# A SwiGLU block on one core: x turned by VectorE in 32x32 blocks, from loads by quarters of its columns

## The chip, the cores and the metric

The kernel runs on one core of a Trainium2 chip. The metric is device time in microseconds. Three runs of the kernel before took 163.49, 163.84 and 164.01 us; their median, 163.84 us, is what the changed kernel is held against. The profiled execution had a span of 162.2 us on core 0, at a granted TensorE clock of 1.000.

## The reference

All tensors are bf16: x is 1 x 2048 x 640, w_gate and w_up are 640 x 1536, w_down is 1536 x 640.

```python
g = silu(x @ w_gate)
u = x @ w_up
return (g * u) @ w_down
```

In what follows S = 2048 is the row count, D = 640 the width, F = 1536 the inner width.

## The kernel before, in words

The rows are worked off in four blocks `sb` of 512. The inner width is cut into KF = 12 chunks `fc` of 128, and the width D into KD = 5 pieces `kd` of 128. The contraction of the first two products runs over D, so x must lie with D on the partitions: the tile `xT` holds it, 128 partitions by 5 by 2048.

For each block and each chunk, `proj` (L193) makes five matmuls into a PSUM tile `pg` (gate) and five into `pu` (up), each with a 128 x 128 weight and 512 columns of `xT`. `gate` (L208) then runs Silu on ScalarE from `pg` into `sg` and multiplies `sg` by `pu` on VectorE into the tile `aT`. The PSUM tiles `pg` and `pu` share four buffers (tag `gu`), so a chunk's matmuls need buffers that the Silu or the multiplication of an earlier chunk has released. `sg` has three buffers.

When a block's twelve chunks are done, the down projection follows. Its last 128 output columns are made transposed in `po_t` (L270), copied by ScalarE to `ot_t`, turned on VectorE into `ot_q` (L281) and stored in four pieces by ScalarE's queue. Its first 512 columns come in four row groups `j`, each twelve matmuls into `po_a` (L299), a copy to `ot` on ScalarE (L308) and a store on SP's queue (L317). `po_a` and `po_t` have two buffers each.

The last T = 4 rows of x are left out of the gate and up matmuls of the last block. VectorE computes them instead, as 96 "dots" (L148), each a product of one turned weight chunk (`wgT` or `wuT`, loaded by the DMA crossbar, L132) with one of these rows (`x_row`, L137), summed along 640 elements. `do_dots(n)` places n dots at points of the loops: two after the gate of a chunk in blocks 1 to 3, except the last two chunks, three before `ot_q`, three after each `po_a` copy with j above 0.

x comes in three ways. Row groups 0 and 1 (128 rows each) are loaded as they are into `x_sb` (L86), turned on TensorE with an identity (`transpose_chunk`, L181) and copied to `xT` (L191). Row groups 2 and 3, and blocks 1, 2 and 3, come through the DMA crossbar straight into `xT` (`turn_x`, L108). Block 1 is asked for after `w_down`; blocks 2 and 3 after block 0's output stores.

The head (L217) is written out by hand: 18 warm-up matmuls `pw` on a tile of ones, the ten transposes, two more warm-ups, then gate matmuls of chunks 0 and 1 by pieces of rows (L237), the up matmuls of rows 0 to 255, and the rest of rows 256 to 511. The order of instructions on TensorE and ScalarE is pinned for the head only; afterwards the scheduler places them. On VectorE and SP, `keep_order` (L98) keeps the written order through the whole kernel. Loads go out on the queues of SP and ScalarE. Their completions use eight semaphores in turn, so a DMA waits for the completion of the one eight before it, whichever of the two queues it was on.

The weights come in chunk groups W_CHUNKS: chunks 0-1, 2-3, 4-7 and 8-11, gate and up each (L83, L120).

Of the kernel before, what the change touches and what calls it, by code (L numbers as in the profile page):

```python
# [7 lines left out]


@with_exitstack  # L10
def _body(
# [8 lines left out]
    nc = tc.nc  # L20
    P = nc.NUM_PARTITIONS
    f32 = mybir.dt.float32
    bf16 = mybir.dt.bfloat16
# [15 lines left out]
    Q = 32  # L39
    N_WARM, N_GAP = 18, 2  # L40
    T = 4
    WT_STEP = 4
    PE_X = 2
    K_CUT = 2
    ROW_J = 0
    W_CHUNKS = [(0, 2), (2, 4), (4, 8), (8, 12)]
    assert D % P == 0 and F % P == 0 and S % S_BLK == 0 and D > DA and SUB == 4

    consts = ctx.enter_context(tc.tile_pool(name="consts", bufs=1))
    work = ctx.enter_context(tc.tile_pool(name="work", bufs=3))  # L50
    outp = ctx.enter_context(tc.tile_pool(name="outp", bufs=3))
    psum = ctx.enter_context(
        tc.tile_pool(name="psum", bufs=2, space=bass.MemoryType.PSUM)
    )

    ident = consts.tile([P, P], bf16)
    x_sb = consts.tile([P, PE_X, D], bf16)
    xT = consts.tile([P, KD, S], bf16)
    wg_sb = consts.tile([P, KD, F], bf16)
    wu_sb = consts.tile([P, KD, F], bf16)  # L60
# [7 lines left out]
    row_s = consts.tile([P, KF, T], f32)  # L68
    prod = consts.tile([P, D], f32)

    make_identity(nc, ident[:])

    x_v = x2.rearrange("(c p) d -> p c d", p=P)
    xt_v = x2.rearrange("s (kd p) -> s kd p", p=P)
    wg_v = w_gate.rearrange("(kd p) f -> p kd f", p=P)
    wu_v = w_up.rearrange("(kd p) f -> p kd f", p=P)
    wd_v = w_down.rearrange("(kf p) d -> p kf d", p=P)

    def wslice(a, b):
        return slice(a * P, b * P)  # L80

    def load_w(eng, dst, src, a, b):
        eng.dma_start(out=dst[:, :, wslice(a, b)], in_=src[:, :, wslice(a, b)])  # L83

    def load_x(eng, c0, c1):
        eng.dma_start(out=x_sb[:, c0:c1, :], in_=x_v[:, c0:c1, :])  # L86

    def issue_order(a, b):
        tc.add_manual_dep(
# [15 lines left out]
    silu_first = consts.tile([P, 1], f32)  # L105
    nc.vector.memset(ones[:], 1.0)  # L106

    def turn_x(c0, c1):  # L108
        s_sl = slice(c0 * P, c1 * P)
        nc.sync.dma_start_transpose(out=xT[:, :, s_sl], in_=xt_v[s_sl])  # L110

    load_x(nc.sync, 0, 1)
    load_x(nc.scalar, 1, 2)
    f_sl = wslice(*W_CHUNKS[0])
    for dst, src, first, second in (
        (wg_sb, wg_v, nc.sync, nc.scalar),
        (wu_sb, wu_v, nc.scalar, nc.sync),
    ):
        for eng, k_sl in ((first, slice(0, K_CUT)), (second, slice(K_CUT, KD))):
            eng.dma_start(out=dst[:, k_sl, f_sl], in_=src[:, k_sl, f_sl])  # L120
    turn_x(PE_X, SUB)
    nc.scalar.activation(silu_first[:], ones[:, 0:1], ACT.Silu)
    for a, b in W_CHUNKS[1:]:
        load_w(nc.sync, wg_sb, wg_v, a, b)
        load_w(nc.sync, wu_sb, wu_v, a, b)
    nc.sync.dma_start(out=wd_sb[:], in_=wd_v)
    wgt_v = w_gate.rearrange("d (kf p) -> d kf p", p=P)
    wut_v = w_up.rearrange("d (kf p) -> d kf p", p=P)

    def turn_w(dst, src):  # L130
        for a in range(0, KF, WT_STEP):
            nc.sync.dma_start_transpose(  # L132
                out=dst[:, a : a + WT_STEP, :], in_=src[:, a : a + WT_STEP, :]
            )

    turn_x(1 * SUB, 2 * SUB)
    nc.sync.dma_start(  # L137
        out=x_row[:],
        in_=x2[S - T : S, :].rearrange("t d -> (t d)").partition_broadcast(P),
# [26 lines left out]

    dots = row_dots()

    def do_dots(n):
        for _ in range(n):  # L170
            next(dots, None)
# [3 lines left out]
    def warm(n):  # L175
        for _ in range(n):
            nc.tensor.matmul(  # L177
                pw[:, 0:P], lhsT=ones[:], rhs=ones[:], start=True, stop=True
            )

    def transpose_chunk(c, parts):  # L181
        c_sl = slice(c * P, (c + 1) * P)
        for copy, tag, k0, k1 in parts:
            pt = psum.tile([P, k1 - k0, P], bf16, tag=tag, name="pt")
            for kd in range(k0, k1):
                nc.tensor.transpose(  # L186
                    out=pt[:, kd - k0, :],
                    in_=x_sb[:, c, kd * P : (kd + 1) * P],
                    identity=ident[:],
                )  # L190
            copy(out=xT[:, k0:k1, c_sl], in_=pt[:])  # L191

    def proj(ps, w_sb, fc, sb, c0, c1):  # L193
        for kd in range(KD):
# [22 lines left out]
    def head():  # L217

        dve, act = nc.vector.tensor_copy, nc.scalar.copy
        split = [(act, "po_a", 0, 2), (dve, "po_b", 2, KD)]
        late = PE_X * P
        (pg0, pu0), (pg1, pu1) = gu_tiles(), gu_tiles()
        warm(N_WARM)
        transpose_chunk(0, split)
        transpose_chunk(1, split)
        warm(N_GAP)  # L230
        early = [(kd, c * P, (c + 1) * P) for c in range(PE_X) for kd in range(K_CUT)]
        early += [(kd, 0, late) for kd in range(K_CUT, KD)]
        for kd, c0, c1 in early:
            for fc, pg in ((0, pg0), (1, pg1)):


                nc.tensor.matmul(  # L237
                    pg[:, c0:c1],
                    lhsT=wg_sb[:, kd, wslice(fc, fc + 1)],
                    rhs=xT[:, kd, c0:c1],  # L240
                    start=(kd == 0 and c0 == 0),
                    stop=(kd == KD - 1),
                )
        proj(pu0, wu_sb, 0, 0, 0, late)
        proj(pu1, wu_sb, 1, 0, 0, late)
        for fc, pg, pu in ((0, pg0, pu0), (1, pg1, pu1)):
            proj(pg, wg_sb, fc, 0, late, S_BLK)
            proj(pu, wu_sb, fc, 0, late, S_BLK)
            gate(pg, pu, 0, fc, S_BLK)
        keep_order(mybir.EngineType.PE)  # L250
        keep_order(mybir.EngineType.Activation)

    head()
    for sb in range(NSB):
        n_s = S_BLK if sb < NSB - 1 else S_BLK - T
        for fc in range(KF):
            if sb == 0 and fc < 2:
                continue
            pg, pu = gu_tiles()
            proj(pg, wg_sb, fc, sb, 0, n_s)  # L260
            proj(pu, wu_sb, fc, sb, 0, n_s)
            gate(pg, pu, sb, fc, n_s)
            if sb > 0 and fc < KF - 2:
                do_dots(2)


        n_t = (SUB if sb < NSB - 1 else SUB - 1) * P
# [12 lines left out]
        do_dots(3)  # L280
        nc.vector.transpose(out=ot_q[:], in_=ot_t[:])  # L281
        for q in range(P // Q):
            nc.scalar.dma_start(
                out=out2[
                    sb * S_BLK : sb * S_BLK + n_t, DA + q * Q : DA + (q + 1) * Q
                ].rearrange("(i r) c -> r i c", r=Q),
                in_=ot_q[q * Q : (q + 1) * Q, :].rearrange("r (i c) -> r i c", c=Q),
            )

        for j in range(SUB):  # L290
            s0 = sb * S_BLK + j * P
            last = sb == NSB - 1 and j == SUB - 1
            cols = [(0, DA, "po_a")]
            if last:
                cols = [(0, DA // 2, "po_a"), (DA // 2, DA, "po_a"), (DA, D, "po_b")]
            for c0, c1, tag in cols:
                po = psum.tile([P, c1 - c0], f32, tag=tag, name="po_a")
                for kf in range(KF):
                    nc.tensor.matmul(  # L299
                        po[:],  # L300
                        lhsT=aT[:, kf, s0 : s0 + P],
                        rhs=wd_sb[:, kf, c0:c1],
                        start=(kf == 0),
                        stop=(kf == KF - 1),
                    )
                ot = outp.tile([P, c1 - c0], bf16, name="ot" if c1 < D else "ot_b")
                if c1 < D:
                    nc.scalar.copy(ot[:], po[:])  # L308
                    eng = nc.sync
                else:  # L310
                    nc.vector.tensor_copy(out=ot[:], in_=po[:])  # L311
                    eng = nc.scalar
                if 0 < j and not last:
                    do_dots(3)
                if sb == NSB - 1 and j == ROW_J:
                    row_tail()
                eng.dma_start(out=out2[s0 : s0 + P, c0:c1], in_=ot[:])  # L317
        if sb == 0:
            turn_x(2 * SUB, 3 * SUB)
            turn_w(wuT, wut_v)  # L320
            turn_x(3 * SUB, 4 * SUB)
    keep_order(mybir.EngineType.DVE)
    keep_order(mybir.EngineType.SP)

# [104 lines left out]
```

## Time and profile before

| What | Value |
|---|---|
| Runs of the kernel before | 163.49, 163.84, 164.01 us; median 163.84 |
| Span of the profiled execution | 162.2 us |
| TensorE matmul busy | 159.8 us, 99% of the span |
| VectorE busy | 110.9 us, 68% |
| ScalarE busy | 42.7 us, 26% |
| DMA packets | 42441, 15.86 MB |
| SP queue | 33536 packets, 37.7% of 16 engines |
| ScalarE queue | 8896 packets, 4.1% of 16 engines |

The profiled execution's own time is recorded as its span from first to last instruction; what lies around it is not in the profile, and the median of the runs is 1.64 us above that span.

The profile's chain of waits is followed back from the last instruction; in this profile it is almost only TensorE. A group's "idle before" is time in which its engine had nothing to do, with what ended it. Times in the timeline are microseconds from the start of the span, and its columns are start, length, engine, line, operation, output and input tiles, shapes and count.

### The profile page before, as it was taken

How to read it: one execution, taken by the hardware profiler on the slowest of the kernel's cores; microseconds unless marked ns; L12 is line 12 of the kernel's file. 1: busy time of each engine (PE TensorE's matmuls, PEld its weight loads, DVE VectorE, ACT ScalarE, POOL GpSimd, SP SyncE). 2: the span in 40 equal slices, each digit the busy share in tenths (PEclk: the TensorE clock that was granted, in tenths of full speed). 3: DMA queues.
4: the chain of work that ended last, by engine and by line, in shares of the span. 5: the costliest groups of instructions: out<-in, count | busy, mean ns of one | idle time of the engine just before them, and what ended most of it. 6: DMA issues, size and time to landing. Idle time of an engine off the chain costs nothing.

```text
span 162.2 us, 2118 instructions
## 1 busy us (share of the span) xinstructions
PE 159.8 (99%) x798; PEld 77.9 (48%) x798; DVE 110.9 (68%) x249; ACT 42.7 (26%) x74; POOL 0.6 (0%) x6
## 2 busy tenths in 40 slices
PE   9999999999999999999999999999999999999995
PEld 8854444444444444444444444444444444445454
DVE  2042233599469999979919999979964999993000
ACT  5132222112222222221222322221214222222121
POOL 1000000000000000000000000000000000000000
PEclk9999999999999999999999999999999999999999
DMA  7999999994179992003110000000320000000312
GB/s 208 258 339 348 362 218 249 219 234 94 34 185 178 224 195 61 4 0 34 65 65 0 0 4 2 0 0 2 63 69 32 0 0 0 0 0 4 50 39 73
DMA packets 42441, 15.86 MB, mean 98 GB/s; under 512 B 33216, under 2 KB 42304, under 8 KB 42432
## 3 DMA queue, kind: packets, MB, share of 16 engines
q1 hardware_dynamic: 33536, 14.72, 37.7%
q10 hardware_dynamic: 8896, 1.02, 4.1%
q8 instruction: 6, 0.10, 0.2%
q14 instruction: 3, 0.02, 0.1%
HBM read 6.88 MB, written 2.62 MB: 59 GB/s over the span
## 4 chain that ended last, share of the span: by engine, by line
PE 99%; DVE 0%; issue 0%
PE pu L195 32%; PE pg L195 31%; PE po_a L299 26%; PE po_t L270 6%; PE pw L177 1%; PE pg L237 1%; PE pt L186 1%; DVE ot_b L311 0%; DVE ones L106 0%
## 5 line engine op out<-in xcount | busy, mean ns | idle before, releaser
L195 PE MATMUL pu<-xT,wu_sb 128*128 128x512 bf16 (+2 forms) x250 | 59.8, 370 | 0.0
L195 PE MATMUL pg<-xT,wg_sb 128*128 128x512 bf16 (+2 forms) x240 | 58.5, 374 | 0.0
L213 DVE TENSOR_TENSOR aT<-sg,pu 128x512 bf16<-128x512 f32 (+1 forms) x48 | 32.8, 683 | 32.8 <-PE pu L195 28.1
L212 ACT ACTIVATE sg<-pg 128x512 f32<-128x512 f32 (+1 forms) x48 | 28.6, 596 | 71.2 <-PE pg L195 68.1
L299 PE MATMUL po_a<-wd_sb,aT 128*128 128x512 bf16 (+2 forms) x216 | 42.8, 358 | 0.0
L148 DVE SCALAR_TENSOR_TENSOR prod<-wgT,x_row 128x640 f32<-128x640 bf16 x48 | 39.4, 821 | 1.1
L148 DVE SCALAR_TENSOR_TENSOR prod<-wuT,x_row 128x640 f32<-128x640 bf16 x48 | 39.4, 822 | 1.0
L195 PEld LDWEIGHTS <-wu_sb 128*128 128x128 bf16 x250 | 24.4, 98 | 27.6 <-DMA wu_sb<-in_w_up_dram 0.3
L195 PEld LDWEIGHTS <-wg_sb 128*128 128x128 bf16 x240 | 23.5, 98 | 26.9
L299 PEld LDWEIGHTS <-aT 128*128 128x128 bf16 x216 | 20.7, 98 | 21.6
L308 ACT CAST ot<-po_a 128x512 bf16<-128x512 f32 (+1 forms) x17 | 9.5, 560 | 32.0 <-PE po_a L299 20.8
L270 PE MATMUL po_t<-aT,wd_sb 128*128 128x512 bf16 (+1 forms) x48 | 10.4, 366 | 0.0
L270 PEld LDWEIGHTS <-wd_sb 128*128 128x128 bf16 x48 | 4.7, 98 | 5.1
L311 DVE CAST ot_b<-po_a 128x128 bf16<-128x128 f32 x1 | 0.3, 291 | 9.9 <-PE po_a L299 9.9
L279 ACT CAST ot_t<-po_t 128x512 bf16<-128x512 f32 (+1 forms) x4 | 2.2, 558 | 11.6 <-PE po_t L270 11.6
L148 DVE DVE_READ_ACCUMULATOR prod<-wuT,x_row 128x1 f32 x48 | 3.9, 82 | 0.0
L148 DVE DVE_READ_ACCUMULATOR prod<-wgT,x_row 128x1 f32 x48 | 3.9, 82 | 0.0
L281 DVE STREAM_TRANSPOSE ot_q<-ot_t 128x512 bf16<-128x512 bf16 (+1 forms) x4 | 2.7, 678 | 1.7 <-ACT ot_t L279 1.7
L177 PE MATMUL pw<-ones 128*128 128x128 bf16 x20 | 2.5, 313 | 0.4 <-DVE ones L106 0.4
L191 DVE COPY xT<-pt 128x384 bf16<-128x384 bf16 x2 | 0.7, 358 | 2.9 <-PE pt L186 2.9
L237 PE MATMUL pg<-xT,wg_sb 128*128 128x128 bf16 (+1 forms) x14 | 2.3, 360 | 0.0
L177 PEld LDWEIGHTS <-ones 128*128 128x128 bf16 x20 | 2.1, 148 | 0.4 <-DVE ones L106 0.4
(15 smaller groups left out, 7.6 us busy)
## 6 DMA issues: line engine op xcount, KB each, us to landing
wd_sb<-in_w_down_dram SPq DMA_DIRECT2D x1, 1920.0 KB, 14.5
out_dram<-ot SPq DMA_DIRECT2D x15, 128.0 KB, 1.7
wg_sb<-in_w_gate_dram SPq DMA_DIRECT2D x2, 640.0 KB, 7.7
wu_sb<-in_w_up_dram SPq DMA_DIRECT2D x2, 640.0 KB, 8.7
x_row<-in_x_dram SPq DMA_DIRECT2D x1, 640.0 KB, 4.7
out_dram<-ot_q ACTq DMA_DIRECT2D x12, 32.0 KB, 1.9
wg_sb<-in_w_gate_dram SPq DMA_DIRECT2D x1, 320.0 KB, 4.9
wu_sb<-in_w_up_dram SPq DMA_DIRECT2D x1, 320.0 KB, 5.4
```

The source lines that it names most:

```text
L148: nc.vector.scalar_tensor_tensor(out=prod[:], in0=wT[:, fc, :], scalar=1.0, in1=x_row[:, t, :], op0=ALU.mult, op1=ALU.mult, accum_out=acc[ ...
L177: nc.tensor.matmul(pw[:, 0:P], lhsT=ones[:], rhs=ones[:], start=True, stop=True)
L186: nc.tensor.transpose(out=pt[:, kd - k0, :], in_=x_sb[:, c, kd * P : (kd + 1) * P], identity=ident[:],)
L195: nc.tensor.matmul(ps[:, c0:c1], lhsT=w_sb[:, kd, fc * P : (fc + 1) * P], rhs=xT[:, kd, sb * S_BLK + c0 : sb * S_BLK + c1], start=(kd == 0 ...
L212: nc.scalar.activation(sg[:, 0:n_s], pg[:, 0:n_s], ACT.Silu)
L213: nc.vector.tensor_tensor(out=aT[:, fc, s0 : s0 + n_s], in0=sg[:, 0:n_s], in1=pu[:, 0:n_s], op=ALU.mult)
L237: nc.tensor.matmul(pg[:, c0:c1], lhsT=wg_sb[:, kd, wslice(fc, fc + 1)], rhs=xT[:, kd, c0:c1], start=(kd == 0 and c0 == 0), stop=(kd == KD ...
L270: nc.tensor.matmul(po_t[:], lhsT=wd_sb[:, kf, DA:D], rhs=aT[:, kf, sb * S_BLK : sb * S_BLK + n_t], start=(kf == 0), stop=(kf == KF - 1),)
L279: nc.scalar.copy(ot_t[:], po_t[:])
L281: nc.vector.transpose(out=ot_q[:], in_=ot_t[:])
L299: nc.tensor.matmul(po[:], lhsT=aT[:, kf, s0 : s0 + P], rhs=wd_sb[:, kf, c0:c1], start=(kf == 0), stop=(kf == KF - 1),)
L308: nc.scalar.copy(ot[:], po[:])
```

## The change

All of x now goes one way. It is loaded by quarters of its columns: quarter q, columns 160q to 160q+159, goes to partitions 32q to 32q+31, with row r of every 32-row group on partition 32q + r. One packet is 160 elements, 320 bytes. VectorE's block transpose (32 x 32 elements in each quarter of the partitions) then turns it into `xT`. It reads every fifth element of the 160, so partition p of piece k of `xT` is column 5p + k of x, and the gate and up weights are loaded with the matching row order (`(p kd) f`).

Row group 0 is in `xq_00`, row group 1 in `xq_01`, row groups 2 and 3 in `xq_02`; blocks 1 to 3 are `xq_1`, `xq_2`, `xq_3`. Block 0's quarters are loaded on both queues, two each; the other blocks' on SP's queue: block 1 before the weights of chunks 8-11, block 2 before `w_down`, block 3 after it. The turns of block 0 stand in the head. Those of blocks 1 and 2 stand behind the gates of block 0's chunks 5, 6, 7 and 9, 10, 11; those of block 3 in block 0's down projection, between the dots. Up weights of chunks 0-1 come in one load on SP's queue instead of two on both. The identity, the transposes on TensorE, their copies and the crossbar loads of x are gone. The 20 warm-ups all stand ahead of the first real matmul, and the gate matmuls of rows 0 to 255 go by row groups of 128 columns.

```diff
-    N_WARM, N_GAP = 18, 2
+    QN = P // Q
+    QD = D // QN
+    N_WARM = 20
-    ident = consts.tile([P, P], bf16)
-    x_sb = consts.tile([P, PE_X, D], bf16)
+    xq_0 = [consts.tile([P, SUB, QD], bf16, name=f"xq_0{c}") for c in range(2)]
+    xq_0.append(consts.tile([P, 2 * SUB, QD], bf16, name="xq_02"))
+    xq_n = [consts.tile([P, S_BLK // Q, QD], bf16, name=f"xq_{b}") for b in range(1, NSB)]
-    wg_v = w_gate.rearrange("(kd p) f -> p kd f", p=P)
-    wu_v = w_up.rearrange("(kd p) f -> p kd f", p=P)
+    wg_v = w_gate.rearrange("(p kd) f -> p kd f", kd=KD)
+    wu_v = w_up.rearrange("(p kd) f -> p kd f", kd=KD)
...
+    def load_quarter(eng, xq, q, s0, n):
+        eng.dma_start(
+            out=xq[q * Q : (q + 1) * Q],
+            in_=x2[s0 : s0 + n, q * QD : (q + 1) * QD].rearrange("(b r) j -> r b j", r=Q),
+        )
+
+    def turn(xq, s0, n, k0, k1):
+        src = xq[:].rearrange("p b (c kd) -> p kd b c", kd=KD)
+        for kd in range(k0, k1):
+            nc.vector.transpose(out=xT[:, kd, s0 : s0 + n], in_=src[:, kd])
...
+    load_halves(xq_0[0], 0, P)
+    load_first(nc.sync, wg_sb, wg_v, 0, K_CUT)
+    load_first(nc.scalar, wg_sb, wg_v, K_CUT, KD)
+    load_halves(xq_0[1], P, P)
+    load_first(nc.sync, wu_sb, wu_v, 0, KD)
+    load_halves(xq_0[2], 2 * P, 2 * P)
...
+    def load_block(i):
+        for q in (0, 2, 1, 3):
+            load_quarter(nc.sync, xq_n[i - 1], q, i * S_BLK, S_BLK)
+
+    for n, (a, b) in enumerate(W_CHUNKS[1:]):
+        if n == 2:
+            load_block(1)
         load_w(nc.sync, wg_sb, wg_v, a, b)
         load_w(nc.sync, wu_sb, wu_v, a, b)
+    load_block(2)
     nc.sync.dma_start(out=wd_sb[:], in_=wd_v)
+    load_block(3)
...
-    turn_x(1 * SUB, 2 * SUB)
...
+    def late_turns():
+        for i in range(1, NSB):
+            for kd in range(KD):
+                turn(xq_n[i - 1], i * S_BLK, S_BLK, kd, kd + 1)
+                yield
...
+    TURNS = {5: 2, 6: 2, 7: 1, 9: 2, 10: 2, 11: 1}
...
+        turn(xq_0[0], 0, P, 0, K_CUT)
+        turn(xq_0[0], 0, P, K_CUT, KD)
+        turn(xq_0[1], P, P, 0, K_CUT)
+        turn(xq_0[1], P, P, K_CUT, KD)
+        turn(xq_0[2], late, late, 0, KD)
...
-            if sb > 0 and fc < KF - 2:
+            if sb == 0:
+                do_turns(TURNS.get(fc, 0))
+            elif fc < KF - 2:
                 do_dots(2)
...
+                if sb == 0:
+                    do_turns(2 if j == 0 else 1)
                 if 0 < j and not last:
                     do_dots(3)
...
         if sb == 0:
-            turn_x(2 * SUB, 3 * SUB)
             turn_w(wuT, wut_v)
-            turn_x(3 * SUB, 4 * SUB)
```

In the changed kernel the gate multiplication stands at L231, a turn of x at L93, a quarter's load at L85, the dots at L164 and `proj` at L213.

More of the change, by code (lines that the diff above doesn't have):

```diff
@@ L6 @@
 from concourse._compat import with_exitstack
-from concourse.masks import make_identity
 @with_exitstack
@@ L39, in _body @@
     Q = 32
-    N_WARM, N_GAP = 18, 2
+    QN = P // Q
+    QD = D // QN
+    N_WARM = 20
     T = 4
     WT_STEP = 4
-    PE_X = 2
     K_CUT = 2
@@ L69, in _body @@
     prod = consts.tile([P, D], f32)
-    make_identity(nc, ident[:])
-    x_v = x2.rearrange("(c p) d -> p c d", p=P)
-    xt_v = x2.rearrange("s (kd p) -> s kd p", p=P)
-    wg_v = w_gate.rearrange("(kd p) f -> p kd f", p=P)
-    wu_v = w_up.rearrange("(kd p) f -> p kd f", p=P)
+    wg_v = w_gate.rearrange("(p kd) f -> p kd f", kd=KD)
+    wu_v = w_up.rearrange("(p kd) f -> p kd f", kd=KD)
     wd_v = w_down.rearrange("(kf p) d -> p kf d", p=P)
@@ L83, in load_w @@
         eng.dma_start(out=dst[:, :, wslice(a, b)], in_=src[:, :, wslice(a, b)])
-    def load_x(eng, c0, c1):
-        eng.dma_start(out=x_sb[:, c0:c1, :], in_=x_v[:, c0:c1, :])
+    def load_quarter(eng, xq, q, s0, n):
[7 more added lines that the diff above has]
+            nc.vector.transpose(out=xT[:, kd, s0 : s0 + n], in_=src[:, kd])
     def issue_order(a, b):
@@ L106, in _body, with load_first, load_halves @@
     nc.vector.memset(ones[:], 1.0)
[L108 to L113, printed above, removed]
-    f_sl = wslice(*W_CHUNKS[0])
[L115 to L121, printed above, removed]
-    nc.scalar.activation(silu_first[:], ones[:, 0:1], ACT.Silu)
-    for a, b in W_CHUNKS[1:]:
+    f_sl = wslice(*W_CHUNKS[0])
+    def load_first(eng, dst, src, k0, k1):
+        eng.dma_start(out=dst[:, k0:k1, f_sl], in_=src[:, k0:k1, f_sl])
+    def load_halves(xq, s0, n):
+        for q in range(QN // 2):
+            load_quarter(nc.sync, xq, q, s0, n)
+            load_quarter(nc.scalar, xq, q + QN // 2, s0, n)
+    load_halves(xq_0[0], 0, P)
[4 more added lines that the diff above has]
+    load_halves(xq_0[2], 2 * P, 2 * P)
+    nc.scalar.activation(silu_first[:], ones[:, 0:1], ACT.Silu)
+    def load_block(i):
[4 more added lines that the diff above has]
+            load_block(1)
         load_w(nc.sync, wg_sb, wg_v, a, b)
         load_w(nc.sync, wu_sb, wu_v, a, b)
+    load_block(2)
     nc.sync.dma_start(out=wd_sb[:], in_=wd_v)
+    load_block(3)
     wgt_v = w_gate.rearrange("d (kf p) -> d kf p", p=P)
@@ L167, in _body, with do_turns @@
     dots = row_dots()
+    def late_turns():
[3 more added lines that the diff above has]
+                yield
+    turns = late_turns()
+    def do_turns(n):
+        for _ in range(n):
+            next(turns, None)
+    TURNS = {5: 2, 6: 2, 7: 1, 9: 2, 10: 2, 11: 1}
     def do_dots(n):
@@ L179, in warm @@
             )
[L181 to L191, printed above, removed]
     def proj(ps, w_sb, fc, sb, c0, c1):
@@ L217, in head @@
     def head():
-        dve, act = nc.vector.tensor_copy, nc.scalar.copy
-        split = [(act, "po_a", 0, 2), (dve, "po_b", 2, KD)]
-        late = PE_X * P
+        late = 2 * P
         (pg0, pu0), (pg1, pu1) = gu_tiles(), gu_tiles()
         warm(N_WARM)
[L228 to L243, printed above, removed]
+        turn(xq_0[0], 0, P, 0, K_CUT)
[3 more added lines that the diff above has]
+        turn(xq_0[2], late, late, 0, KD)
+        for c in range(2):
+            for kd in range(KD):
+                for fc, pg in ((0, pg0), (1, pg1)):
+                    nc.tensor.matmul(
+                        pg[:, c * P : (c + 1) * P],
+                        lhsT=wg_sb[:, kd, wslice(fc, fc + 1)],
+                        rhs=xT[:, kd, c * P : (c + 1) * P],
+                        start=(kd == 0 and c == 0),
+                        stop=(kd == KD - 1 and c == 1),
+                    )
         proj(pu0, wu_sb, 0, 0, 0, late)
```

## The prediction, made before the changed kernel ran

> **What bounds the kernel now.** First the page: busy shares, then the chain that ended last.
>
> ```profile
> PE 159.8 (99%) x798; PEld 77.9 (48%) x798; DVE 110.9 (68%) x249; ACT 42.7 (26%) x74; POOL 0.6 (0%) x6
> PE 99%; DVE 0%; issue 0%
> ```
>
> TensorE is the chain from end to end: nothing else can shorten the run, and any wait put into its row lengthens it one for one. So two questions: when does steady work begin, and does any later wait enter. The timeline of TensorE answers the first.
>
> ```profile
> 2.29 1.31 PE L186 MATMUL pt<-ident,x_sb 128*128 128x128 bf16 x10
> 3.61 2.34 PE L237 MATMUL pg<-xT,wg_sb 128*128 128x128 bf16 x14
> 5.80 1.29 PE L195 MATMUL pu<-xT,wu_sb 128*128 128x256 bf16 x10
> 9.11 1.24 PE L195 MATMUL pg<-xT,wg_sb 128*128 128x512 bf16 x5
> ```
>
> The gate/up pair of chunk fc 2 starts at 9.11; from there a group of five matmuls comes each 1.08 us. The second question is VectorE's, in its timeline around the first down projection (po_t starts at 30.69, po_a ends at 43.64):
>
> ```profile
> 33.29 0.82 DVE L148 SCALAR_TENSOR_TENSOR prod<-wgT,x_row 128x640 f32<-128x640 bf16 x1
> 34.10 0.71 DVE L281 STREAM_TRANSPOSE ot_q<-ot_t 128x512 bf16<-128x512 bf16 x1
> 34.73 0.78 DVE L148 SCALAR_TENSOR_TENSOR prod<-wgT,x_row 128x640 f32<-128x640 bf16 x1
> ...
> 42.38 0.08 DVE L148 DVE_READ_ACCUMULATOR prod<-wgT,x_row 128x1 f32 x1
> 46.07 0.69 DVE L213 TENSOR_TENSOR aT<-sg,pu 128x512 bf16<-128x512 f32 x1 [3.61 <-PE pu L195]
> 48.29 0.68 DVE L213 TENSOR_TENSOR aT<-sg,pu 128x512 bf16<-128x512 f32 x1
> 50.50 0.68 DVE L213 TENSOR_TENSOR aT<-sg,pu 128x512 bf16<-128x512 f32 x1
> ```
>
> VectorE is full from 31.57 to 42.4, rests 3.61 us, then needs 2.21 us for each chunk (a gate and two dots) while TensorE needs 2.16. Its one reserve is that rest. The queue of SP is the third view:
>
> ```profile
> 10.73 12.88 SPq L110 DMA_TRANSPOSE xT<-in_x_dram  x1
> 23.66 0.58 SPq L137 DMA_DIRECT2D x_row<-in_x_dram  x1
> 24.28 10.66 SPq L132 DMA_TRANSPOSE wgT<-in_w_gate_dram  x3
> ```
>
> x_row lands 4.7 us after issue (28.4), the first wgT 5.6 (29.9), just before the dots.
>
> **The head.** Gone: ten PE transposes, four copies, two gap matmuls (two warm-ups move ahead). The front warm-ups end near 2.6, then TensorE waits. Added: twelve small loads and fifteen turns. Every DMA in the built program waits for the one eight before it, on either queue, and SP's are in order, so the later quarters are late:
> - xq_00: x_sb took 2.2 and 2.7 us to land; issues are 0.46 apart, so its last quarter is there at 2.6. wg's first chunk (2.8 and 3.6 us to landing) is issued 0.4 later than now: 3.6 to 4.2. xq_01's second quarters wait for first ones: issue 2.1, landing 4.4.
> - A turn: 0.712 for 512 columns and 0.578 for 384 give 0.17 plus 1.05 ns per column: 0.31 for 128, 0.44 for 256. Back to back they come 0.08 closer (34.10 to 34.73 is 0.63): 0.23 and 0.36. Chunk 1 is turned and multiplied by 5.7; wu, now one SP load after these, lands about 5.8 as now. The ten pu matmuls end at 6.9.
> - xq_02: its quarters wait for wg's pieces, SP's stand behind wu; issues 2.7 to 4.7, landing 6.9 by 2.2 each. Moving 1.31 MB in the head agrees: 512-byte packets ran at about 290 GB/s (28 ns per packet and engine), 1024-byte ones at 350 (47 ns), and the 8896 packets of ACT's queue, mostly 64 bytes, took 4.1% of 16 engines: 12 ns. A line through these gives 21 ns for the new 320-byte packet; 2048 of x and 1280 of w over 16 engines are 5.0 us, after 1.3 of latency.
> - kd 0 of xq_02 is turned at 7.3, kd 4 at 8.75 (four times 0.36 later); then one matmul and fifteen of 0.108: fc 2 starts at 10.5. I take 10.7, as quarters may collide, so **the head costs 1.6**. Bounds: landing at 6.0 gives 0.6; landing at 7.6, with the last groups still at the slow pace of L237 (0.21 per 256 columns, against 0.108 later, perhaps because of the new gaps), gives 3.8.
>
> [...]
>
> **Blocks 1 to 3.** Three crossbar loads of x leave SP and twelve quarters come, all ahead of x_row. Per block: 2048 packets of 21 ns over 16 engines are 2.7 us; a wgT crossbar load of the same bytes takes 10.66/3 = 3.55. Weights for chunks 8 to 11 and wd go back by one and two blocks. wd, landing at 23.4 now, comes near 29; needed at 36 (below). W(8,12), landed at 16.4 now, comes by 20 and is needed near 24. Turns of blocks 1 and 2 (0.63 each, one or two behind a gate) fit in VectorE's 1.47 idle per chunk. wgT moves from 29.9 by two blocks more (5.4 to 7.1), less 1.5 blocks faster than crossbar (0 to 1.3): 34.0 to 37.0. Limit: three dots (2.6) must be done before ot_q near 41, so 38.5. Not binding, with one to four us in hand; past that point every us is a us of TensorE. wuT is issued earlier. SP's stores of sb 0's outputs stand behind the wgT issues, now done near 40 instead of 34.9, and po_a's first output is ready only near 43; ACT's four stores of ot_q now stand behind its third output copy: no cost from either.
>
> **Where the stall arises.** The built program's order shows a thing the diff doesn't: TensorE now runs five groups of sb 1 (pg, pu of fc 0, fc 1, pg of fc 2) ahead of sb 0's po_t, while VectorE keeps the written order: three dots, ot_q, five turns of xq_3 and nine dots mixed, and only then the gate of sb 1's fc 0. With all times plus the head's delay:
> - po_t starts at 30.69 + 5 x 1.08 = 36.1. In the row ot_q ends 4.04 after po_t's start: 40.1. Five turns are 3.15, nine dots (0.867 apart) 7.8: the gate of fc 0 starts at 51.0, done 51.65.
> - TensorE ends po_a at 36.1 + 2.59 + 10.36 = 49.05, does pu of fc 2 and pg of fc 3, and at 51.2 needs that gate's buffer for pu of fc 3: **stall 0.45**.
> - Gates then come each 2.21: fc 1 done 53.9 against 53.8 (0.1), fc 2 done 56.1 against 55.0, where fc 5's pg needs it: **1.1**. Fc 6 to 11 wait 0.05 each, the difference of 2.21 and 2.16: 0.3. The next po_t waits for the gates of fc 10 and 11 (74.5 against 74.0): 0.5.
> Sum 2.45. So VectorE's rest of 3.61 is eaten by po_t's 5.4 us later start, plus 3.15 of turns. After sb 1 VectorE has caught up, and blocks 2 and 3 are as now; the cover there is thin but unchanged.
>
> **The sum.** 162.2 span + 1.6 + 2.45 = 166.25. The median of the three runs is 163.84, 1.64 above that span; on it the forecast is 167.9. With the head's bounds and a tenth either way on turns and dots, this case alone spans 166.5 to 170.5.
>
> **The rivals.**
> - *Late wgT.* If 320-byte packets cost 1.6 times my line (34 ns), a block takes 4.35 instead of 2.7, and four blocks stand ahead of wgT: 6.6 more on 35.5 (the middle) is 42.1. VectorE's three dots, queued ahead of ot_q, then end at 44.7; ot_q, the turns and sb 1's first gate behind them go back by 3.0 from 41.1 plus the head's extra 0.6, and TensorE waits for that gate: 167.9 + 3.0 + 0.6 = 171.5. Each further us is paid whole. [...] Against: 64-byte packets at 12 ns. Chance 0.19.
> - *Slow turns.* The turn reads every fifth element; ot_q reads neighbours. At twice the 1.05 ns per column, a 512 turn is 0.54 dearer, five of them 2.7 in the stall, and five of 256 1.35 in the head: 167.9 + 4.05 = 171.9. [...] No trace here shows a strided turn. Chance 0.14.
> - *Cheap turns, early x: faster.* If a turn of 512 came each 0.25 (the DVE copy of 384 columns took 0.358), 1.9 leaves VectorE's chain, all sb 1 stalls vanish, and the head is 0.4: 164.2, no change. If xq_02 also lands before 5.9, fc 2 starts ahead of 9.11; at 5.6 it starts at 8.2: 162.9. The point: turns under 0.3 and landing under 5.9 together. Against: ot_q is the same operation and shape, and 1.31 MB won't be there at 5.6. Chance 0.07 in all, 0.04 of it faster, 0.03 no change.
> - That the change isn't what it says is excluded: the built order has no crossbar load of x and no PE transpose.
>
> **Numbers.** Main case 0.60, at 167.9. A measurement of this kernel tells about 0.3% (0.5 us) from no change. Range 166.0 to 172.4: it leaves out the cheap case and the far ends of the two dear ones, about 0.2. Slower 0.93.
>
> **What would show it.** Right: fc 2 near 10.7; VectorE turning xq_02 while TensorE waits; sb 1's first gate near 52.6; TensorE idle before pu of fc 3 and more before pg of fc 5, put down to L231's gates; DVE near 100% from 41 to 76. Wrong: first dot later than 40 (late wgT); L93 turns of 512 over 0.9 (slow) or under 0.4 (cheap); no TensorE idle between 50 and 76.

## The result, and the profile after

The changed kernel takes 170.23 us (median of four runs, 169.54 to 170.53) against 163.67 us (163.16 to 164.01) for the kernel before: 1.040 times as long, interval 1.037 to 1.043. The forecast of 167.9 us had the sign and, of its two losses, one almost exactly; the other was over two and a half times as large as forecast. The profiled execution took 170.52 us with a span of 168.7. One run in all that follows, of the last experiment's kernel, took 166.96 us, more than 1.5% above the fastest of its kernel, and is left out of that kernel's numbers.

Busy shares, and the chain that ended last:

```profile
PE 162.5 (96%) x794; PEld 78.3 (46%) x794; DVE 123.7 (73%) x277; ACT 42.0 (25%) x72; POOL 0.2 (0%) x4
PE 73%; DVE 16%; issue 5%; DMA 4%; ACT 0%; ACTq 0%; DVEq 0%
```

The chain was 99% TensorE; now a fifth of it is VectorE and DMA. TensorE's timeline (start, length, then in brackets the idle time before and what ended it) shows where:

```profile
4.44 1.27 PE L254 MATMUL pg<-xT,wg_sb 128*128 128x128 bf16 x10 [1.74 <-DMA wg_sb<-in_w_gate_dram]
6.07 1.23 PE L254 MATMUL pg<-xT,wg_sb 128*128 128x128 bf16 x10 [0.35 <-DVE xT L93]
7.66 2.31 PE L213 MATMUL pu<-xT,wu_sb 128*128 128x256 bf16 x10 [0.37 <-DMA wu_sb<-in_w_up_dram]
...
13.33 1.24 PE L213 MATMUL pg<-xT,wg_sb 128*128 128x512 bf16 x5
...
60.10 1.24 PE L213 MATMUL pg<-xT,wg_sb 128*128 128x512 bf16 x5 [0.97 <-DVE aT L231]
...
78.39 0.38 PE L289 MATMUL po_t<-aT,wd_sb 128*128 128x512 bf16 x1 [0.22 <-DVE aT L231]
78.60 5.34 PE L318 MATMUL po_a<-wd_sb,aT 128*128 128x512 bf16 x24
```

The second block's po_a in the kernel before (the listing ends at 82):

```profile
72.13 10.09 PE L299 MATMUL po_a<-wd_sb,aT 128*128 128x512 bf16 x46
```

Two marks split the loss. The gate matmuls of fc 2 start at 13.33 instead of 9.11: **the head costs 4.22**. The second block's first po_a starts at 78.60 instead of 72.13, 6.47 late: **block 1 adds 2.25**. The span grew by 6.5, so nothing is lost or won after that.

VectorE's timeline shows the two places from the other side:

```profile
3.56 1.12 DVE L93 STREAM_TRANSPOSE xT<-xq 128x128 bf16<-128x128 bf16 x5 [3.23 <-DMA xq<-in_x_dram]
5.70 1.13 DVE L93 STREAM_TRANSPOSE xT<-xq 128x128 bf16<-128x128 bf16 x5 [1.02 <-DMA xq<-in_x_dram]
8.81 1.85 DVE L93 STREAM_TRANSPOSE xT<-xq 128x256 bf16<-128x256 bf16 x5 [1.99 <-DMA xq<-in_x_dram]
...
40.22 0.83 DVE L164 SCALAR_TENSOR_TENSOR prod<-wgT,x_row 128x640 f32<-128x640 bf16 x1 [3.69 <-DMA wgT<-in_w_gate_dram]
...
43.71 0.71 DVE L300 STREAM_TRANSPOSE ot_q<-ot_t 128x512 bf16<-128x512 bf16 x1 [0.92 <-ACT ot_t L298]
44.35 1.99 DVE L93 STREAM_TRANSPOSE xT<-xq 128x512 bf16<-128x512 bf16 x3
...
54.95 0.68 DVE L231 TENSOR_TENSOR aT<-sg,pu 128x512 bf16<-128x512 f32 x1
```

In the head the turns wait for x each time; the last of them ends at 10.66. In the down projection VectorE waits 3.69 us for wgT, then 0.92 for `ot_t`, the copy of TensorE's po_t, and from 43.71 on has no idle time until it gives TensorE the gate it has been waiting for. The rest of 3.61 us that stood here before is gone.

The chain listed in order of time says why the head is late:

```profile
0.55 2.81 DMA xq<-in_x_dram
3.36 0.02 issue
3.38 4.24 DMA wu_sb<-in_w_up_dram
7.62 0.04 issue
7.66 2.31 PE pu L213 x10
9.97 1.11 PE pg L213 x5
```

wu is issued only at 3.38, when a quarter issued at the start has landed (each DMA waits for the one eight before it), and lands 4.24 later. Ten up matmuls then run at twice their later time (0.21 us each for 256 columns, against 0.108 from about 12.5 on), so the chain goes by wu and that pace. The turns of the last rows are as late: the last of them ends at 10.66, and TensorE's matmul behind it starts at 10.72, 0.1 later than its pace alone would have it. The queue of SP goes on:

```profile
4.86 0.82 SPq L85 DMA_DIRECT2D xq<-in_x_dram  x2
...
23.57 7.28 SPq L85 DMA_DIRECT2D xq<-in_x_dram  x4
30.89 1.55 SPq L153 DMA_DIRECT2D x_row<-in_x_dram  x1
32.49 11.20 SPq L149 DMA_TRANSPOSE wgT<-in_w_gate_dram  x3
```

The quarters of xq_02 go out at 4.86, when the second piece of wg has landed; the last block's four loads occupy SP for 7.28, and wgT's issue begins at 32.49 instead of 24.28.

### The profile page after: what moved, and what is told of

It is laid out like the page before. It is cut to its first block, busy times and chain, and to the rows that moved or that the text cites. A ratio compares the mean times of both kernels' runs of the same rounds, so it can differ in the third digit from the quotient of the medians.

```text
span 168.7 us, 2163 instructions
## 1 busy us (share of the span) xinstructions
PE 162.5 (96%) x794; PEld 78.3 (46%) x794; DVE 123.7 (73%) x277; ACT 42.0 (25%) x72; POOL 0.2 (0%) x4
## 4 chain that ended last, share of the span: by engine, by line
PE 73%; DVE 16%; issue 5%; DMA 4%; ACT 0%; ACTq 0%; DVEq 0%
PE pu L213 25%; PE pg L213 25%; PE po_a L318 19%; DVE prod L164 10%; PE po_t L289 4%; DVE aT L231 4%; DMA wu_sb<-in_w_up_dram 3%; DVE xT L93 2%; DMA xq<-in_x_dram 2%; ACT ot_t L298 0%; ACTq L85 0%; DVE ot_b L330 0%; DVEq L93 0%; DVE ot_q L300 0%; DVEq L164 0%
## 5 line engine op out<-in xcount | busy, mean ns | idle before, releaser
L213 PE MATMUL pu<-xT,wu_sb 128*128 128x512 bf16 (+2 forms) x250 | 61.3, 379 | 0.5 <-DMA wu_sb<-in_w_up_dram 0.4
L213 PE MATMUL pg<-xT,wg_sb 128*128 128x512 bf16 (+2 forms) x240 | 59.5, 378 | 1.0 <-DVE aT L231 1.0
L231 DVE TENSOR_TENSOR aT<-sg,pu 128x512 bf16<-128x512 f32 (+1 forms) x48 | 32.7, 683 | 18.7 <-PE pu L213 18.0
L164 DVE SCALAR_TENSOR_TENSOR prod<-wgT,x_row 128x640 f32<-128x640 bf16 x48 | 39.3, 820 | 4.7 <-DMA wgT<-in_w_gate_dram 3.7
L164 DVE SCALAR_TENSOR_TENSOR prod<-wuT,x_row 128x640 f32<-128x640 bf16 x48 | 39.4, 821 | 1.0
L213 PEld LDWEIGHTS <-wu_sb 128*128 128x128 bf16 x250 | 25.0, 100 | 29.0 <-issue 0.7
L213 PEld LDWEIGHTS <-wg_sb 128*128 128x128 bf16 x240 | 23.9, 100 | 28.9 <-issue 2.3
L93 DVE STREAM_TRANSPOSE xT<-xq 128x512 bf16<-128x512 bf16 (+2 forms) x30 | 14.7, 534 | 6.2 <-DMA xq<-in_x_dram 6.2
L289 PE MATMUL po_t<-aT,wd_sb 128*128 128x512 bf16 (+1 forms) x48 | 10.6, 366 | 0.2 <-DVE aT L231 0.2
L254 PE MATMUL pg<-xT,wg_sb 128*128 128x128 bf16 x20 | 2.5, 306 | 2.1 <-DMA wg_sb<-in_w_gate_dram 1.7
L164 DVE DVE_READ_ACCUMULATOR prod<-wgT,x_row 128x1 f32 x48 | 3.9, 82 | 0.0
L164 DVE DVE_READ_ACCUMULATOR prod<-wuT,x_row 128x1 f32 x48 | 3.9, 81 | 0.0
L254 PEld LDWEIGHTS <-wg_sb 128*128 128x128 bf16 x20 | 2.0, 138 | 2.6 <-DMA wg_sb<-in_w_gate_dram 2.0
```

The source lines that it names most:

```text
L93: nc.vector.transpose(out=xT[:, kd, s0 : s0 + n], in_=src[:, kd])
L164: nc.vector.scalar_tensor_tensor(out=prod[:], in0=wT[:, fc, :], scalar=1.0, in1=x_row[:, t, :], op0=ALU.mult, op1=ALU.mult, accum_out=acc[ ...
L213: nc.tensor.matmul(ps[:, c0:c1], lhsT=w_sb[:, kd, fc * P : (fc + 1) * P], rhs=xT[:, kd, sb * S_BLK + c0 : sb * S_BLK + c1], start=(kd == 0 ...
L231: nc.vector.tensor_tensor(out=aT[:, fc, s0 : s0 + n_s], in0=sg[:, 0:n_s], in1=pu[:, 0:n_s], op=ALU.mult)
L254: nc.tensor.matmul(pg[:, c * P : (c + 1) * P], lhsT=wg_sb[:, kd, wslice(fc, fc + 1)], rhs=xT[:, kd, c * P : (c + 1) * P], start=(kd == 0 a ...
L289: nc.tensor.matmul(po_t[:], lhsT=wd_sb[:, kf, DA:D], rhs=aT[:, kf, sb * S_BLK : sb * S_BLK + n_t], start=(kf == 0), stop=(kf == KF - 1),)
```

## The experiments

"Head" below is the start of fc 2 less 9.11, "block 1" the delay that the second block's first po_a has beyond it; both are from the profiled execution. Kernels that share a head differ in it from one profile to the next (12.34 to 13.80), so the head's size in the changed kernel is 3.2 to 4.7, and a head that falls between these two, in one profile of another kernel, shows no gain by itself.

**1. Is block 1's loss the chain on VectorE?** Block 3 is turned before the dots instead of among them:

```diff
-    TURNS = {5: 2, 6: 2, 7: 1, 9: 2, 10: 2, 11: 1}
+    TURNS = {5: 2, 6: 2, 7: 1, 9: 2, 10: 2, 11: 6}
...
-                if sb == 0:
-                    do_turns(2 if j == 0 else 1)
```

> The five turns of block 3 move from block 0's down projection to directly behind block 0's last gate, ahead of the first three dots; loads and the order on TensorE stay. In the changed kernel VectorE idles 3.69 us there, until wgT lands at 40.22, and xq_3 should have landed near 36.5. Theory VectorE chain (what stands behind ot_q sets sb 1's first gate): five turns of 0.64 leave that chain, the gate of fc 0 starts near 51.9 instead of 54.95, all waits in sb 1 vanish, span 168.7 - 2.25 = 166.4. Rival late loads (the DMA queues set sb 1's wait): the same 168.7, since no load moves. If xq_3 lands later than 37.0, the dots start later than 40.2 and part of the gain is lost.

167.71 us (167.67 to 167.77), 1.024 [1.022, 1.026]. Head 3.78, block 1 0.09. VectorE's timeline:

```profile
37.07 3.30 DVE L93 STREAM_TRANSPOSE xT<-xq 128x512 bf16<-128x512 bf16 x5 [0.97 <-issue]
41.56 0.83 DVE L164 SCALAR_TENSOR_TENSOR prod<-wgT,x_row 128x640 f32<-128x640 bf16 x1 [1.20 <-DMA wgT<-in_w_gate_dram]
```

The same five turns now fill time in which VectorE would have waited for wgT. So block 1's 2.25 is the work queued behind ot_q, and moving 3.15 us of it takes the loss away. The 166.4 us that was expected is a span, and the profiled execution's was 166.1; the head of this profile is 0.44 smaller than the changed kernel's, block 1 accounts for the rest.

**2. Is it TensorE's order?** The prediction counted five groups of block 1 that the scheduler runs ahead of block 0's po_t. Here TensorE keeps the written order:

```diff
+    keep_order(mybir.EngineType.PE)
     keep_order(mybir.EngineType.DVE)
```

> The order on TensorE is pinned to the written one, so block 0's po_t comes before all of block 1's gate and up groups; nothing else is changed. Rival early groups (the five groups ahead of po_t cause sb 1's wait): 2.25 us of waits go, span 166.4. Theory VectorE chain with late wgT behind it: po_t is 5.4 us earlier but the first dot still waits for wgT until 40.2, so ot_q ends at 43.4, the first gate starts near 54.1 and is needed by TensorE at 53.3 (43.64 + 4.22 + 5 groups); 1.5 us of wait, then 0.05 a chunk and 0.5 at the end: span 168.4 to 168.8, no change.

170.42 us (169.79 to 171.82), 1.042 [1.037, 1.047]: no change, and a span of 168.7 as expected. The head of this profile is 4.69, the largest of all, and block 1 adds 1.45. po_t now starts at 35.38 instead of 40.30, and the same place is held by something else:

```profile
40.88 0.83 DVE L164 SCALAR_TENSOR_TENSOR prod<-wgT,x_row 128x640 f32<-128x640 bf16 x1 [3.88 <-DMA wgT<-in_w_gate_dram]
...
43.37 0.71 DVE L300 STREAM_TRANSPOSE ot_q<-ot_t 128x512 bf16<-128x512 bf16 x1
```

ot_q runs straight behind the dots that waited for wgT, at 43.37 where it was 43.71. So two things each keep VectorE's chain back to about the same time: po_t's late place and wgT's late landing. Taking away the first shows the second; experiment 6 will take away the second alone.

**3 and 4. Why is wgT late?** On the pinned order, blocks 1 to 3 are loaded in as many loads of as many bytes, first with the same 320-byte packets but spread over all 128 partitions, then as whole rows of 1280 bytes. (The elements of x then stand in another order.)

```diff
-            load_quarter(nc.sync, xq_n[i - 1], q, i * S_BLK, S_BLK)
+            nc.sync.dma_start(
+                out=xq_n[i - 1][:, q * SUB : (q + 1) * SUB, :],
+                in_=x2[i * S_BLK : (i + 1) * S_BLK, q * QD : (q + 1) * QD].rearrange(
+                    "(b r) j -> r b j", r=P
+                ),
+            )
```
```diff
-            load_quarter(nc.sync, xq_n[i - 1], q, i * S_BLK, S_BLK)
+            nc.sync.dma_start(
+                out=xq_n[i - 1][:, q * SUB : (q + 1) * SUB, :].rearrange("p b j -> p (b j)"),
+                in_=x2[i * S_BLK + q * P : i * S_BLK + (q + 1) * P, :],
+            )
```

> Blocks 1 to 3 are loaded with as many packets of 320 bytes in as many DMAs, but each DMA goes to all 128 partitions instead of 32 (so x's elements of these blocks stand in other places than the products need; this part of the result is another one); TensorE's order is pinned, so the kernel to hold it against is the pinned one. Theory ports (a DMA into 32 partitions is slow): a block loads at about 240 GB/s instead of about 200, wgT lands 2 us or more before 40.2, span at least 1.5 below the pinned kernel's. Theory packets (320 bytes are slow wherever they go): wgT lands within 0.5 of 40.2, the same time as pinned.

> Blocks 1 to 3 are loaded as whole rows, 1280 bytes to each of 128 partitions, in as many DMAs of as many bytes (x's elements of these blocks stand in other places than the products need); TensorE's order is pinned. Both theories on the loads: at 350 GB/s a block takes 1.9 us, wgT lands near 36, the first gate of sb 1 is ready before TensorE needs it, 2 us below the pinned kernel's time. If wgT still lands near 40, neither packets nor ports are it, but the number of DMAs and their waits for the one eight before.

Over 128 partitions: 167.79 us (167.40 to 168.76), 1.026 [1.022, 1.029], head 3.57, block 1 nothing. Whole rows: 167.47 us (167.21 to 168.25), 1.024 [1.020, 1.027], head 3.23, block 1 nothing. SP's issue of wgT, in the pinned kernel, the one over 128 partitions and the one by whole rows:

```profile
32.68 11.70 SPq L149 DMA_TRANSPOSE wgT<-in_w_gate_dram  x3
```
```profile
30.10 10.53 SPq L154 DMA_TRANSPOSE wgT<-in_w_gate_dram  x3
```
```profile
23.68 15.65 SPq L152 DMA_TRANSPOSE wgT<-in_w_gate_dram  x3
```

The first dot over 128 partitions:

```profile
37.36 0.83 DVE L169 SCALAR_TENSOR_TENSOR prod<-wgT,x_row 128x640 f32<-128x640 bf16 x1 [1.47 <-DMA wgT<-in_w_gate_dram]
```

SP reaches block 1's loads at 8.80, 8.96 and 8.40, so the difference arises in the blocks. From there to wgT's issue it took 22.7 to 24.8 us in every kernel with quarters, 21.1 here and 21.3 in experiment 5 over 128 partitions, and 15.3 by whole rows. Going to 32 partitions costs 2.6 us of wgT's issue, and 3.5 of its landing (first dot at 37.36 instead of 40.88); packets of 320 bytes instead of 1280 cost 6.4 more. The landing of a 160 KB load fell from 7.5 to 6.1 us with the partitions alone; by whole rows it was 7.2, so one load's landing time does not tell how fast a queue moves on. SP's queue held 38.0% of 16 engines over 168.7 us, and 33.6% over 165.8 with 128 partitions: 134 us of engine time less, 22 ns for each of the 6144 packets if all of it is theirs. The prediction had 21 ns for the whole packet.

**5 and 6. Is the head held by partitions, or by the number of loads?** First all loads of x, the head's too, over 128 partitions (on the pinned order, x's elements again in another order); then the changed kernel's own layout with rows 0 to 255 in four loads of 80 KB instead of eight of 40, and wu directly behind wg.

```diff
-            out=xq[q * Q : (q + 1) * Q],
-            in_=x2[s0 : s0 + n, q * QD : (q + 1) * QD].rearrange("(b r) j -> r b j", r=Q),
+            out=xq[:, q * (n // P) : (q + 1) * (n // P), :],
+            in_=x2[s0 : s0 + n, q * QD : (q + 1) * QD].rearrange("(b r) j -> r b j", r=P),
```
```diff
-    load_halves(xq_0[0], 0, P)
+    load_halves(xq_0[0], 0, 2 * P)
     load_first(nc.sync, wg_sb, wg_v, 0, K_CUT)
     load_first(nc.scalar, wg_sb, wg_v, K_CUT, KD)
-    load_halves(xq_0[1], P, P)
     load_first(nc.sync, wu_sb, wu_v, 0, KD)
...
```

> Every load of x, block 0's too, keeps its packets of 320 bytes, its size and its place in the queues, but goes to 128 partitions (x's elements stand in other places than the products need); TensorE's order is pinned, so it stands against the kernel with 128 partitions for blocks 1 to 3 alone (167.8). Theory ports: block 0's quarters move at 250 GB/s or more instead of 120 to 190, the first row group is turned from 2.6 instead of 3.1 to 3.5, the last rows from 7.5 instead of 8.6, fc 2 a us earlier, time near 166.8. Theory waits: the holes stay, fc 2 within 0.4 of 12.7.

> Rows 0 to 255 come in four quarter loads of 80 KB instead of eight of 40 KB, and wu is asked for right behind wg; so no early load has to wait for one that comes late. The rest is the changed kernel. Theory waits for the one eight before (in the changed kernel the DMA engines stand at 0.2 to 0.5 of their time at 2.5 to 2.75 and at 4.75 to 5.5): the holes close, xq's last rows are turned from near 7.3 instead of 8.81, wu lands before 7, fc 2 starts at 11.5 to 12.3 instead of 13.3, time 1.0 to 1.8 below the changed kernel's 170.2. Theory ports alone (32 partitions are slow): as many bytes at the same 150 to 190 GB/s, fc 2 within 0.5 of 13.3, no gain.

Over 128 partitions: 167.35 us (167.16 to 167.69), 1.025 [1.022, 1.027], head 3.48; experiment 3's kernel, which it stands against, has 3.57. Row group 0 is turned from 3.69, there from 3.03 and in the changed kernel from 3.56. So in the head the partitions are not the cause. Four loads: 169.45 us (169.14 to 169.61), 1.037 [1.035, 1.039], head 3.47. TensorE has no wait for wu (7.14 instead of 7.66), but the last rows are still turned only from 8.95. fc 2 starts at 12.58, where 11.5 to 12.3 was expected. The median is 0.8 us lower, but the intervals of the two ratios overlap and the head lies among those of the changed kernel, so a gain isn't shown. That the weights' transfers, asked for in the meantime, keep back these rows is argued here and shown for whole rows in experiment 11.

This kernel also completes experiment 2. wgT lands earlier, the order on TensorE is the changed kernel's, and `ot_q` waits for po_t's copy alone:

```profile
38.24 0.83 DVE L162 SCALAR_TENSOR_TENSOR prod<-wgT,x_row 128x640 f32<-128x640 bf16 x1 [2.45 <-DMA wgT<-in_w_gate_dram]
...
42.97 0.71 DVE L298 STREAM_TRANSPOSE ot_q<-ot_t 128x512 bf16<-128x512 bf16 x1 [2.16 <-ACT ot_t L296]
```

Block 1 still adds 2.28. So the early groups hold block 1 alone (2.28), late wgT holds it alone (1.45, behind a larger head), and with neither, in experiments 3 to 5, nothing is left.

What the small loads do is seen in quarter-microsecond windows (engines' busy time, granted clock, the DMA engines' share, GB/s), first of the changed kernel, then of the kernel before:

```profile
1.75:2.00 0.25, 0.25 (x5) 0.25 (x4) 0.00 (x0) 0.00 (x0) 0.00 (x0) 1.00 0.68 146
2.50:2.75 0.25, 0.21 (x2) 0.00 (x0) 0.00 (x0) 0.00 (x0) 0.00 (x0) 1.00 0.22 18
```
```profile
1.75:2.00 0.25, 0.25 (x6) 0.25 (x4) 0.00 (x0) 0.25 (x1) 0.00 (x0) 1.00 1.01 340
```

The DMA engines run dry: their share is 0.68 and then 0.22, where it was 1.01. A load of x takes 0.44 us to issue; by an estimate from that time and its 40 KB, two queues can ask for at most some 180 GB/s, and then a load waits for the one eight before: SP's queue 0.9 us for a quarter, ahead of wu, and 0.8 for wg, ahead of xq_02.

**7, 8 and 9. Is it TensorE's slow pace?** Until about 12.5 us a 256-column matmul of the changed kernel takes 0.21, and 0.108 later. More matmuls on the tile of ones fill TensorE's gaps, first in the changed kernel (38 in front instead of 20, four behind each row group), then after another repair of the loads: all of block 0 in four 160 KB loads ahead of the weights, with experiment 1's early turns, without and with 44 in front.

```diff
-    N_WARM = 20
+    N_WARM, N_FILL = 38, 4
...
+            warm(N_FILL if c else 0)
...
+        warm(N_FILL)
```
```diff
-    load_halves(xq_0[0], 0, P)
+    load_halves(xq_0, 0, S_BLK)
...
-    load_halves(xq_0[1], P, P)
...
-    load_halves(xq_0[2], 2 * P, 2 * P)
```
```diff
-    N_WARM = 20
+    N_WARM = 44
```

> TensorE's waits in the changed kernel's head are filled with warm-up matmuls: 38 ahead instead of 20, and four more behind each row group of 128; nothing else is changed. Theory slow pace from gaps (256 columns took 0.21 until near 12 in the changed kernel and 0.108 from 5.8 on in the kernel before): the fast pace is there before 7.7, the ten first up matmuls take 1.1 instead of 2.1, fc 2 starts near 12.4, time 0.5 to 1.0 below 170.2, with less spread. Rival (the pace does not matter, the turns and loads set it): fc 2 stays at 13.3.

> Against the kernel with early turns (167.7): block 0 comes in four quarter loads of 160 KB, two on each queue, ahead of wg and wu, instead of twelve of 40 and 80 KB between them; the turns keep their sizes. Theory small loads (each 40 KB load costs its queue 0.45 us of issue, so two queues move at most 180 GB/s, and later ones wait for the one eight before): with seven early loads nothing waits, x has landed at 4.5 to 5.0, the last rows are turned by 9 instead of 11.1, fc 2 starts at 10.6 to 11.6 instead of 12.9, time 165.4 to 166.5. Rival ports or packets (32 partitions, 320 bytes: 640 KB at 150 to 190 GB/s is there only at 5 to 5.5 and wg and wu wait behind it): wu lands at 8 or later, fc 2 near 12.9, no gain.

> The kernel with four loads for block 0 and 44 warm-up matmuls instead of 20, so that TensorE is busy until about 5.1. Theory pace (now that x is early, the slow pace of TensorE sets the head): the up matmuls of rows 0 to 255 and all behind them run at 0.108 per 256 columns, fc 2 starts 0.7 to 1.2 earlier than with 20 warm-ups. Rival turns: the turns end near 9 in both, fc 2 within 0.4 of the kernel with 20.

Filled alone: 170.31 us (169.42 to 171.14), 1.043 [1.037, 1.047], no gain (0.5 to 1.0 was expected). The profile is of the fastest of its four runs, 169.42. In it the pace is high early (the ten pu take 1.27 where they took 2.31), but wu lands at 8.1 and the last turns run from 9.09 to 10.93 and fc 2 follows them, at 12.72. Four loads: 166.79 us (166.20 to 167.25), 1.020 [1.017, 1.024], against 1.024 [1.022, 1.026] for experiment 1's kernel: a gain isn't clear. All x is there at 5.27 and turned by 9.13, but now the pace is what is late:

```profile
5.64 2.29 PE L249 MATMUL pg<-xT,wg_sb 128*128 128x128 bf16 x20 [2.93 <-DVE xT L92]
7.73 2.34 PE L210 MATMUL pu<-xT,wu_sb 128*128 128x256 bf16 x10
```

and fc 2 starts at 12.85, where 10.6 to 11.6 was expected. The profile is of the slowest of the four runs; the spans of two others were 0.8 and 1.0 us shorter. Four loads and filled: 165.17 us (165.11 to 165.22), 1.011 [1.008, 1.013], fc 2 at 10.75:

```profile
7.37 1.25 PE L210 MATMUL pu<-xT,wu_sb 128*128 128x256 bf16 x10
```

So late x and the slow pace stand in for each other: mending the pace alone gave nothing, mending the loads alone left fc 2 where it was (12.89 in experiment 1's profile), and with the loads mended the pace is worth 1.6 us of the median and 2.1 of fc 2's start in the two profiles, where 0.7 to 1.2 was expected. No run of either kernel falls among those of the other.

**10 and 11. The head as it was before.** With experiment 1's early turns, block 0 goes back to whole rows and TensorE transposes (row groups 2 and 3 as well, where the kernel before used the crossbar), their columns taken by steps of five so that `xT` keeps the changed layout. In the second, these rows are asked for ahead of wu.

```diff
-    load_halves(xq_0[0], 0, P)
+    load_rows(nc.sync, 0)
+    load_rows(nc.scalar, 1)
...
-        turn(xq_0[2], late, late, 0, KD)
+        transpose_chunk(0, split)
...
-    load_first(nc.scalar, wu_sb, wu_v, 0, K_CUT)
-    load_first(nc.sync, wu_sb, wu_v, K_CUT, KD)
     load_rows(nc.sync, 2)
     load_rows(nc.scalar, 3)
+    load_first(nc.scalar, wu_sb, wu_v, 0, K_CUT)
+    load_first(nc.sync, wu_sb, wu_v, K_CUT, KD)
```

The first two hunks lead from the changed kernel to the first of the two; the third, in which the weights move behind the rows, leads from the first to the second.

> Block 0 is loaded by whole rows to 128 partitions and turned on TensorE (twenty transposes, reading every fifth column), blocks 1 to 3 as in the kernel with early turns. All theories: the head's 4.2 is undone but for ten more transposes (0.11 each at the slow pace, 0.05 at the fast): fc 2 starts at 9.7 to 10.4, sb 1 has no wait, span 162.9 to 163.5, time 164.3 to 165.0. If the head were slow because of the other order of the weights' rows or of later weights, fc 2 would stay near 12.

> Against the kernel that turns block 0 on TensorE (165.6; there rows 256 to 511 landed only at 7.5 and TensorE waited 1.56 us): the loads of these rows go ahead of wu's. Theory landing order: they land by 5.5, wu near 6.5, TensorE waits at most 0.6 instead of 1.56, fc 2 starts at 10.0 to 10.6 instead of 11.38, time 164.4 to 165.0. Rival (the transposes and their copies set it): fc 2 within 0.3 of 11.4.

The first: 165.60 us (164.78 to 166.19), 1.013 [1.010, 1.017], fc 2 at 11.38 instead of the expected 9.7 to 10.4, because TensorE waits for the late rows:

```profile
7.51 0.75 PE L224 MATMUL pt<-ident,x_sb 128*128 128x128 bf16 x10 [1.56 <-DMA x_sb<-in_x_dram]
```

The second has no such wait:

```profile
5.62 0.72 PE L224 MATMUL pt<-ident,x_sb 128*128 128x128 bf16 x10
...
9.71 1.24 PE L231 MATMUL pg<-xT,wg_sb 128*128 128x512 bf16 x4
```

It takes 164.39 us (five runs, 163.99 to 164.90), 1.006 [1.004, 1.008]. fc 2 starts at 9.71, expected from 10.0 on; head 0.60, block 1 nothing. With a head of this kind and the early turns, then, blocks 1 to 3 by quarters and turns on VectorE cost nothing that shows on TensorE; 0.95 of the 6.56 us between the medians is left. No kernel tried was faster than the kernel before.

## Why the prediction was right, and where it was off

**The head: the term that was mis-sized, 1.6 forecast, 4.22 measured,** beyond its own upper bound of 3.8 in this profile. The turns were sized right: spacings of 0.21, 0.35 and 0.64 for 128, 256 and 512 columns against 0.23, 0.36 and 0.63. What failed is the step that gave each small load the 2.2 us of x_sb's whole rows. The quarters of xq_00 took 2.0 to 2.8 us to land, those of xq_01 3.3 to 3.8, the 80 KB ones 2.9 to 3.5. The 1.3 us of latency in its sum of packets is near what the profile before shows: there the DMA engines' share is 0.00 until 1.00 us and 1.01 from 1.50 to 2.00. And since wu waits for a quarter and xq_02 for wg, whose pieces took 3.5 and 3.8 instead of 2.8 and 3.6, the delay was paid again behind them: row group 0 was turned from 3.56 instead of 2.6, wu was used at 7.66 instead of 5.8, and xq_02 from 8.81 instead of 6.9. wu was also given too little by itself: some 3 us, from an issue behind xq_01's at 2.1 to 5.8, where its loads took 4.7 in the kernel before; it took 4.24, from 3.38. The end of the last turn, forecast at 8.75, was 10.66: 1.9 of the 2.6 that were missing. The other 0.7 is the slow pace between 9.77 and 12.5, which the prediction named but kept for its bound. It can be counted by wu too, which was 1.9 late and was followed by the same pace. Why the later quarters took longer than the first is not settled. It is not the destination's partitions alone (experiment 5).

**Block 1: 2.45 forecast, 2.25 measured.** ot_q ended at 44.42, which is the forecast 40.1 plus the head within 0.1, and the first gate followed 10.53 later instead of 10.9. TensorE's gaps came where they were placed: 0.27 ahead of pu of fc 3 (0.45), 0.05 (0.1), 1.13 ahead of pg of fc 5 (1.1), 0.36 for the six chunks behind it (0.3) and 0.49 at po_t (0.5). Experiment 1 shows the turns in that chain to be the cause. The early groups on TensorE are the reason in the kernel as built, by a margin of 0.92 us; they are not needed for a loss, as experiment 2 shows, since late wgT, the rival, stood right behind them. That this term came out so close is therefore in part luck. The measured 170.23 lies just under the 170.5 to which the main case reached with the head's upper bound, and the head was 0.4 beyond that bound: the sum held by little.

**Blocks 1 to 3 and wgT.** 2.7 us per block was too low: SP issued wgT 8.2 us later than before, and it took 7.6 to land instead of the 5.6 that was assumed. The first dot came at 40.22, past the forecast 34 to 37 and past the limit of 38.5. But the limit moved with the head, by 2.6 beyond forecast, to 41.1. The 0.92 us that ot_q then waited for ot_t is the 0.9 left between the two. wd, forecast at 29, landed at 33.0, needed at 40.3: no cost, as said. wuT was to be issued earlier and was issued at 54.49, before at 47.44; no engine waited for it.

**The rivals.** *Late wgT* came true in its premise, not in its price: late by 3 to 6 us, hidden by the head's own delay and by the early groups of TensorE, and binding once these are pinned. The 34 ns per packet behind its price no run shows by itself; experiment 3 shows 22 ns more per packet over 32 partitions than over 128, if all of that difference is theirs. *Slow turns* is dead, and with it *cheap turns*. The groups of the turns of `xT`, by steps of five elements, and of `ot_q`, of neighbours (behind the first bar busy us and mean ns, behind the second the idle time before them):

```profile
L93 DVE STREAM_TRANSPOSE xT<-xq 128x512 bf16<-128x512 bf16 x15 | 10.5, 732 | 0.0
...
L300 DVE STREAM_TRANSPOSE ot_q<-ot_t 128x512 bf16<-128x512 bf16 x3 | 2.1, 710 | 0.9 <-ACT ot_t L298 0.9
```

The 10-byte step costs 3% (732 ns against 710). The factor of two behind the price of *Slow turns* no run shows; the trace has 1.03 in its place.

**The 32 partitions of a quarter's load.** The forecast had no term for them. In the blocks they cost time: spreading the same packets over 128 partitions brought wgT 3.5 us forward (first dot at 37.36 instead of 40.88). With quarters and weights in flight together, the windows of 4 us between 13 and 33 us show 246 to 319 GB/s in the changed kernel, 229 to 311 in the pinned one and 265 to 379 in the one over 128 partitions. In the head they decided nothing: it was 3.48 with all of x over 128 partitions and 3.57 with block 0 still in 32 (experiment 5).

## What to carry to other kernels

A load that is cut into small pieces is not priced by its bytes: count the issue time per piece (here 0.44 us for 40 KB) and the number of pieces that must land before the next may be asked for, because a delay is paid again at each such link (here 0.9 us ahead of wu and 0.8 ahead of xq_02). Work added to an engine that is not the bottleneck belongs where that engine waits anyway; the same five turns cost 2.25 us in one place and 0.1 in another. When a wait doesn't move after its cause is removed, look for a second cause at the same place before giving up the first.

## What the runs showed of the hardware

- The granted clock stood at 1.00 throughout, also in the windows where a matmul took twice its later time (256 columns in 0.21 us, later in 0.108); the slow pace is visible only in the durations. With the same head it ended anywhere between about 10.7 and 12.9 us, a spread of 2 us; in experiment 7, without the gaps in front, before 5. What else sets that moment no run here shows.
- VectorE's block transpose reads elements by steps of 10 bytes at 732 ns for 512 columns, against 710 for neighbours.
- A DMA of 40 KB took 0.44 us to issue and 2.0 to 3.8 to land, the first ones in the head soonest; 160 KB of whole rows, in the kernel before, landed in 2.2 to 2.7.
